# Softmax attention for one query, forward and backward: the block order of turns 3 to 14 used from turn 1 on

## The chip, the cores and the metric

The kernel runs on one core of a Trainium2 chip. The metric is device time in microseconds (us); lower is better. A core has TensorE (matrix products; PE in the profile, PEld its weight loads), VectorE (DVE), ScalarE (ACT), GpSimd (POOL), SyncE (SP), and data engines that move bytes between HBM and the on-chip memory SBUF. TensorE writes to PSUM, from which VectorE and ScalarE read.

## The reference

There are 32 heads, one query per head, 8192 keys and values per head, 128 wide, all in bf16.

```python
B, H, Sq, Skv, Dh = 1, 32, 1, 8192, 128
...
scores = jnp.einsum('bhqd,bhkd->bhqk', q, k) * scale
attn = _softmax(scores, axis=-1)
return jnp.einsum('bhqk,bhkd->bhqd', attn, v)
```

The outputs are this result and, for a given grad_out, the gradients of q, k and v. With p the softmax of one head, dV is the outer product of p and grad_out, dp is V times grad_out, ds is p times (dp minus the sum of p times dp) times the scale, dq is ds times K, and dK is the outer product of ds and q. So K and V (67 MB each) are read once, and dK and dV, as large, are written once.

## The kernel before, in words

A **turn** takes two heads: one tile of K and one of V, each 128 partitions by 128 rows by 128 values (4 MB). There are 16 turns, 0 to 15. Three SBUF buffers hold K and two hold V; dK and dV are written over K and V in place (`outer`, line 371) and stored from there. The order of the instructions on every engine is the order in which they are written, since the kernel has a manual schedule.

A turn t goes through these steps:

- `k_block(t, c)`, c from 0 to 7 (lines 196 to 209): VectorE transposes an eighth of K in blocks of 32 by 32 (line 200, into one of three buffers XK), and TensorE multiplies it by q in four matmuls of 512 columns (line 208), which add up the scores in PSUM. These blocks are done at the end of turn t - 1.
- `s_back`, `s_top`, `s_exp`, `s_sum`, `p_of` (lines 212 to 255): VectorE turns the scores back (sT, line 215), and the maximum, the exponentials and their sum go to and fro between VectorE, ScalarE and TensorE until p is there.
- dp from V. The old way is `v_part` (lines 260 to 279): TensorE transposes four squares of 128 by 128 (line 273, f32 words) into a PSUM bank, and ScalarE copies the bank to SBUF (line 279); 16 such parts make a turn, and `v_scores` (line 290) multiplies each quarter by grad_out in 8 narrow matmuls of 32 columns of weights. The other way is `v_block` (line 298): VectorE transposes an eighth of V in blocks of 32 by 32, and `v_wide` (line 310) multiplies it in four wide matmuls with the weights do_wide, which `weights_wide` (line 195, four copies on ScalarE) sets for each turn. Four blocks r = 0 to 3 and two quarters of `v_part` then make the whole of V.
- `contract(t, "p")` (line 349) multiplies p with V on TensorE, for the output.
- `v_back` (dpT, line 319), `pd_sum`, `ds_of` (lines 330 to 340): ds; ScalarE writes it to the window win_ds (line 244) that `contract(t, "ds")` uses as weights, to multiply ds with K for dq.
- `outer(t, "p", r)` writes dV, r from 0 to 7, in the same turn; `outer(t - 1, "ds", r)` writes dK of the turn before. Both are on VectorE, at line 371.
- Every fourth turn `gather` (lines 357 to 365) brings an output together: that of p in turns 3, 7, 11 and 15, that of ds in turns 4, 8 and 12 and at the end.

`wide(t)` (line 257) says which turns take the four blocks by VectorE: 3 to 14. It also chooses between two orders of a turn. In the order of **blocks** (from line 479 on) all of the eight multiplications for dK, and seven of those for dV, are done before dpT; the eighth stands between dpT and ds; the store of V is issued ahead of ds; then all of the eight `k_block` of the next turn follow. In the **other** order (turns 1, 2 and 15) 16 parts of V go by TensorE. Five of them are done beside `k_block` of the turn before: by line 464 for turn 1, and by the last lines of the loop for a turn that isn't wide. Two or three multiplications for dV stand before ds, and five after it. In turn 2 these five alternate with the `k_block` of turn 3; in turn 1 they stand ahead of those of turn 2. Turn 0 has an order of its own, in `first` (lines 406 to 465).

SP's queue holds all of the large transfers in this order: the store of K of turn t - 1, the store of V of turn t, the load of K of turn t + 2, the load of V of turn t + 2. Each waits for what it needs, and those behind it wait too. A load of K waits for the store of the dK that had its buffer, three turns back; a load of V for the store of dV two turns back.

Of the kernel before, what the change touches and what calls it, by code (L numbers as in the profile page):

```python
# [27 lines left out]
def kernel(  # L28
# [14 lines left out]
    HP = H // 2  # L43
# [39 lines left out]
    def load_k(t, parts=1):  # L83
        load(k, Kt, t, parts)

    def load_v(t, parts=1):
        load(v, Vt, t, parts)
# [40 lines left out]
    def copies(row):  # L128
        four = xkpool.tile([H, 2 * NW, NQ, QD], BF16, tag="XK", name="four")
        for w in range(NW):  # L130
            for e2 in range(2):
                nc.vector.tensor_copy(
                    four[:, 2 * w + e2],
                    rows[:, row, :].rearrange("h (w j e) -> h w e j", w=NW, e=2)[:, w, e2:e2 + 1, :]
                    .to_broadcast([H, NQ, QD]))
        return four

    def columns(four, cols):
        tp = psT.tile([P, 2 * TB, P], BF16, tag="T", name="tp_q")
        for c in range(2 * NW):  # L140
            nc.tensor.transpose(tp[:, c, 0:H], four[:, c].rearrange("h a j -> h (a j)"), ident[0:H, 0:H])
        for s in range(2):
            nc.vector.tensor_copy(
                cols[s * HF:(s + 1) * HF], tp[s * HF:(s + 1) * HF, 0:2 * NW, 0:H].rearrange(
                    "p c (i s) -> p s c i", s=2)[:, s])
# [42 lines left out]
    def weights_do(t):  # L188
        for z in range(2):
            nc.scalar.copy(do_win[z * W:(z + 1) * W, :, :, SL - 2 + z].rearrange("p s e -> p e s"),  # L190
                           do_cols[z * W:(z + 1) * W, :, 2 * t:2 * t + 2])

    def weights_wide(t):
        for a in range(NQ):
            nc.scalar.copy(do_wide[a * QD:(a + 1) * QD, :, a * QD + SL - 1], do_four[a * QD:(a + 1) * QD, :, t])
# [16 lines left out]
    def s_back(t):  # L212
        x = st[t]
        x["sT"] = backs.tile([P, BN, QD], F32, tag="back", name="sT")
        nc.vector.transpose(x["sT"][:].rearrange("p n r -> p (n r)"), x.pop("s")[:])  # L215

    def s_top(t):
        x = st[t]
        mx = small.tile([P, 1], F32, tag="mx")
        nc.vector.reduce_max(mx[:], x["sT"][:, :, 0:NB], axis=AX.XY)  # L220
        top = small.tile([P, 1], F32, tag="top")
        nc.vector.tensor_scalar_mul(top[:], mx[:], scale)  # L222
        nc.tensor.transpose(x["m"][:, 128:256], top[:].to_broadcast([P, P]), ident_f[:])  # L223

    def s_exp(t):
        x = st[t]
        nbias = small.tile([P, 1], F32, tag="nbias")
        for s in range(2):
            a, b = s * HF, (s + 1) * HF
            nc.vector.tensor_reduce(nbias[a:b], x["m"][a:b, 128 + a:128 + b], axis=AX.X, op=ALU.max, negate=True)  # L230
        e = x["e"] = single.tile([P, NT], F32, tag="e", name="e")
        rs = small.tile([P, 1], F32, tag="rs")
        nc.scalar.activation(e[:].rearrange("p (c n) -> p n c", c=NB), x["sT"][:, :, 0:NB], ACT.Exp, bias=nbias[:],  # L233
                             scale=scale, accum_out=rs[:])
        return rs

    def s_sum(t, rs):
        nc.tensor.matmul(st[t]["m"][:, 0:1], lhsT=same[:], rhs=rs[:], start=True, stop=True, skip_group_check=True)  # L238
# [8 lines left out]
    def p_of(t):  # L247
        x = st[t]
        rinv = x["rinv"] = small.tile([P, 1], F32, tag="rinv", name="rinv")
        nc.vector.reciprocal(rinv[:], x["m"][:, 0:1])  # L250
        x["p"] = single.tile([P, NT, R], BF16, tag="prep", name="p_rep")
        nc.scalar.activation(x["p"][:], x["e"][:].unsqueeze(2).to_broadcast([P, NT, R]), ACT.Copy, scale=rinv[:])
        window_in(t, "p", x["p"][:, :, 0])
        x["rs"] = small.tile([P, 1], F32, tag="rs_s", name="rinv_s")
        nc.scalar.mul(x["rs"][:], rinv[:], scale)

    def wide(t):
        return 3 <= t < HP - 1

    def v_bank(t, m):  # L260
        x = st[t]
        z, i = divmod(m, NM // TB)
        if t == 0:
            if i == 0:
                x["XV", z] = k_in[2][:].rearrange("p n d -> p (n d)").bitcast(F32).rearrange(
                    "p (z m s) -> p z m s", z=NZ, s=P)[:, z]
        elif i == 0:
            x["XV", z] = xvpool.tile([P, NM, P], F32, tag="XV", name="XV_sb")[:]
        T_ps = psT.tile([P, TB, P], F32, tag="T", name="T_ps")
        words = Vt[t][:].rearrange("p n d -> p (n d)").bitcast(F32)  # L270
        for j in range(TB):
            at = (i * TB + j) * NZ + z
            nc.tensor.transpose(T_ps[:, j, :], words[:, at * P:(at + 1) * P], ident_f[:])  # L273
        x["T", m] = T_ps

    def v_copy(t, m):
        x = st[t]
        z, i = divmod(m, NM // TB)
        nc.scalar.copy(x["XV", z][:, i * TB:(i + 1) * TB, :], x.pop(("T", m))[:])  # L279
# [46 lines left out]
    def pd_sum(t):  # L326
        x = st[t]
        nc.tensor.matmul(x["m"][:, 1:2], lhsT=same[:], rhs=x["pd"][:], start=True, stop=True, skip_group_check=True)  # L328
# [13 lines left out]
    def contract(t, which, first=0, last=NG):  # L342
        X, pool = (Vt[t], psO) if which == "p" else (Kt[t], psQ)
        if t % ST == 0 and first == 0:
            acc[which] = pool.tile([P, 512], F32, tag="acc", name="acc_" + which)
        at = 0 if which == "p" else (ST - 1 - t % ST) * SL
        for g in range(first, last):
            b = g % NQ
            nc.tensor.matmul(acc[which][b * QD:(b + 1) * QD, :], lhsT=win[which][:, g, at:at + QD],  # L349
                             rhs=X[:, 4 * g:4 * g + 4, :].rearrange("p n d -> p (n d)"),  # L350
                             start=(t % ST == 0 and g < NQ), stop=(t % ST == ST - 1 and g >= NG - NQ),
                             skip_group_check=True)
        if which == "p" and last == NG:
            nc.gpsimd.memset(win["p"][:, :, t % ST * SL:(t % ST + 1) * SL], 0.0)
# [12 lines left out]
    def outer(t, which, r):  # L367
        x = st[t]
        X, row = (Kt[t], 0) if which == "ds" else (Vt[t], 1)
        a, b = r * BN, (r + 1) * BN  # L370
        nc.vector.tensor_tensor(  # L371
            X[:, a:b, :].rearrange("p n (a b) -> p n a b", b=R),
            x[which][:, a:b, :].unsqueeze(2).to_broadcast([P, BN, D // R, R]),
            x["qd"][:, row, :].rearrange("p (a b) -> p a b", b=R).unsqueeze(1).to_broadcast([P, BN, D // R, R]),
            op=ALU.mult)
# [21 lines left out]
    def v_part(t, m):  # L397
        v_bank(t, m)
        v_copy(t, m)

    HALF = NB // 2
# [10 lines left out]
    def first():  # L412

        def at(i, *zs):
            return [z * (NM // TB) + i for z in zs]

        for m in at(0, 0, 1):
            v_part(0, m)
        s_back(0)
        s_top(0)  # L420
        for m in at(0, 2, 3):
            v_part(0, m)
        four = copies(1)
        rs = s_exp(0)
        for m in at(1, 0, 1, 2):
            v_bank(0, m)
        s_sum(0, rs)
        for m in at(1, 0, 1, 2):
            v_copy(0, m)
        p_of(0)  # L430
        ahead = at(1, 3) + at(2, 0, 1)
        for m in ahead:
            v_bank(0, m)
        contract(0, "p", 0, NG // 2)
        for m in ahead:
            v_copy(0, m)
        for r in range(HALF):
            outer(0, "p", r)
        for m in at(2, 2, 3):
            v_part(0, m)  # L440
        contract(0, "p", NG // 2, NG // 4 * 3)
        for r in range(HALF, NB - 2):
            outer(0, "p", r)
        for m in at(3, 0, 1, 2, 3):
            v_part(0, m)
        contract(0, "p", NG // 4 * 3, NG)
        for z in range(NZ):
            v_scores(0, z)
        weights_do(1)
        v_back(0)  # L450
        pd_sum(0)
        columns(four, do_four)
        outer(0, "p", NB - 2)
        ds_of(0)
        contract(0, "ds")
        prepare(1)
        outer(0, "p", NB - 1)
        store(0, "p")
        load_k(2)
        load_v(2)  # L460
        for c in range(NB):
            k_block(1, c)
            if c > HALF:
                v_part(1, c - HALF - 1)
        weights_q(2)

    first()
# [153 lines left out]
```

## Time and profile before

| what | value |
|---|---|
| time, median of 3 runs | 634.3 us (634.27 to 634.5) |
| profiled execution, time | 634.35 us |
| profiled execution, span | 632.5 us |
| VectorE busy | 550.5 us (87%) |
| TensorE matmul busy | 426.6 us (67%) |
| ScalarE busy | 176.2 us (28%) |
| moved by the data engines | 268.92 MB, mean 425 GB/s |
| mean granted clock of TensorE | 0.81 |

The span is the stretch from the first to the last event of the execution; the time has 1.85 us more around it. The granted clock is 1.0 where TensorE runs at full speed and 0.5 at half. The page of the profile gives shares of the whole span; the views that are cut by time show single turns. A wait is written as the idle time of an engine ahead of an instruction, with the instruction or transfer that ended it.

### The profile page before, as it was taken

Reading aid. Unit: us, or ns where it says so; the run is one execution under the profiler, and the core shown is the slowest. Engines: PE = TensorE matmul, PEld = TensorE weight load, DVE = VectorE, ACT = ScalarE, POOL = GpSimd, SP = SyncE. Lnnn points to the kernel's source line nnn. Section 1 sums busy time; section 2 is a strip of 40 time slices with the busy share of each in tenths; the row PEclk is TensorE's granted clock in tenths of the full one; section 3 lists DMA queues with packets and bytes.
Section 4 is the critical chain, followed back from the end, with each engine's and each line's share of the span. In section 5 each row is a group of like instructions: output and inputs, shape, how many; then the busy total and the mean of one; then the engine's idle time right before and its main releaser. Section 6 shows DMA issues by size and latency. Waiting matters only on the chain.

```text
span 632.5 us, 7251 instructions
## 1 busy us (share of the span) xinstructions
PE 426.6 (67%) x2876; PEld 207.7 (33%) x2876; DVE 550.5 (87%) x630; ACT 176.2 (28%) x439; POOL 9.2 (1%) x27
## 2 busy tenths in 40 slices
PE   5868686488475874758747587474875748757870
PEld 2635252144242421323323242231332314223540
DVE  8688987997988979899797997989979799798893
ACT  1616152041240322404124031240412304122530
POOL 2000000000000000000000000000000000000000
PEclk9989697787698776888868877687886878768965
DMA  8999999999999999999999999999999999999997
GB/s 361 434 418 433 431 430 430 433 432 430 431 430 430 434 424 435 428 435 432 434 443 430 429 432 432 428 431 432 431 428 431 430 431 432 430 432 432 411 407 310
DMA packets 11025, 268.92 MB, mean 425 GB/s; under 512 B 1392, under 2 KB 1392, under 8 KB 1392
## 3 DMA queue, kind: packets, MB, share of 16 engines
q1 hardware_dynamic: 10896, 268.46, 99.0%
q8 instruction: 22, 0.36, 0.2%
q14 instruction: 11, 0.09, 0.0%
q10 hardware_dynamic: 96, 0.02, 0.0%
HBM read 134.23 MB, written 134.23 MB: 424 GB/s over the span
## 4 chain that ended last, share of the span: by engine, by line
PE 41%; DVE 40%; issue 7%; ACT 6%; DMA 4%; DVEq 0%; ACTq 0%
DVE K L371 18%; PE T_ps L273 9%; PE dp_ps L310 9%; DVE XK_sb L200 9%; PE acc_ds L349 7%; PE acc_p L349 6%; PE s_ps L208 5%; DVE V L371 5%; DMA K<-in_k_dram 3%; PE dp_ps L290 3%; DVE XV_blk L298 2%; ACT XV_sb L279 2%; ACT win_ds L244 2%; DVE sT L215 2%; DVE dpT L319 1%
## 5 line engine op out<-in xcount | busy, mean ns | idle before, releaser
L200 DVE STREAM_TRANSPOSE XK_sb<-K 128x1024 f32<-128x1024 f32 x128 | 148.6, 1215 | 40.3 <-PE s_ps L208 37.9
L371 DVE TENSOR_TENSOR V<-p_rep,qd 128x2048 bf16<-128x2048 bf16 x128 | 150.8, 1219 | 7.6 <-PE T_ps L273 3.4
L371 DVE TENSOR_TENSOR K<-ds_rep,qd 128x2048 bf16<-128x2048 bf16 x128 | 149.2, 1211 | 0.5
L208 PE MATMUL s_ps<-XK_sb,q_win 128*128 128x512 bf16 x512 | 132.9, 404 | 9.9 <-DVE XK_sb L200 5.8
L279 ACT COPY XV_sb<-T_ps 128x512 f32<-128x512 f32 x144 | 78.2, 589 | 130.4 <-PE T_ps L273 130.3
L273 PE MATMUL T_ps<-ident_f,V 128*128 128x128 f32 x640 | 92.8, 293 | 0.1
L273 PEld LDWEIGHTS T_ps<-ident_f,V 128*128 128x128 f32 x640 | 75.3, 150 | 34.0 <-issue 26.6
L310 PE MATMUL dp_ps<-XV_blk,do_wide 128*128 128x512 bf16 x192 | 62.3, 454 | 31.2 <-DVE XV_blk L298 31.2
L208 PEld LDWEIGHTS <-q_win 128*128 128x128 bf16 x512 | 50.9, 102 | 85.0 <-issue 38.3
L349 PE MATMUL acc_ds<-K,win_ds 128*32 128x512 bf16 x512 | 52.9, 586 | 33.3 <-ACT win_ds L244 33.3
L298 DVE STREAM_TRANSPOSE XV_blk<-V 128x1024 f32<-128x1024 f32 x48 | 55.3, 1208 | 0.0
L223 PE MATMUL m_ps<-ident_f,top 128*128 128x128 f32 x16 | 6.7, 416 | 62.2 <-DVE top L222 62.2
L349 PE MATMUL acc_p<-V,win_p 128*32 128x512 bf16 x512 | 42.7, 428 | 1.6 <-ACT win_p L244 1.6
L310 PEld LDWEIGHTS <-do_wide 128*128 128x128 bf16 x192 | 19.9, 109 | 49.6 <-DVE XV_blk L298 32.2
L349 PEld LDWEIGHTS <-win_ds 128*32 128x32 bf16 x512 | 17.2, 130 | 56.1 <-ACT win_ds L244 31.2
L185 ACT COPY q_win<-q_blk 128x16 bf16<-128x16 bf16 x16 | 4.2, 261 | 108.7 <-PE s_ps L208 108.7
L233 ACT ACTIVATE e<-sT,nbias 128x128 f32<-128x128 f32 x16 | 8.2, 515 | 69.7 <-DVE nbias L230 69.7
L223 PEld LDWEIGHTS m_ps<-ident_f,top 128*128 128x128 f32 x16 | 2.7, 170 | 68.8 <-issue 62.2
L290 PE MATMUL dp_ps<-XV_sb,do_win 128*32 128x512 bf16 x288 | 20.8, 383 | 5.2 <-ACT XV_sb L279 5.0
L238 PE MATMUL m_ps<-rs,same 128*128 128x1 f32 x32 | 8.3, 327 | 18.1 <-ACT e L233 18.1
L244 ACT ACTIVATE win_ds<-ds,rinv_s 64x128 bf16<-64x128 f32 x32 | 12.8, 399 | 27.5 <-DVE ds L336 27.3
L328 PE MATMUL m_ps<-pd,same 128*128 128x1 f32 x32 | 6.1, 260 | 19.8 <-DVE m_ps L322 19.8
(68 smaller groups left out, 215.0 us busy)
## 6 DMA issues: line engine op xcount, KB each, us to landing
K<-in_k_dram SPq DMA_DIRECT2D x15, 4096.0 KB, 19.2
V<-in_v_dram SPq DMA_DIRECT2D x15, 4096.0 KB, 19.3
out_dram<-V SPq DMA_DIRECT2D x15, 4096.0 KB, 25.4
out_dram<-K SPq DMA_DIRECT2D x14, 4096.0 KB, 27.4
out_dram<-K SPq DMA_DIRECT2D x4, 2048.0 KB, 9.5
K<-in_k_dram SPq DMA_DIRECT2D x4, 1024.0 KB, 8.2
V<-in_v_dram SPq DMA_DIRECT2D x4, 1024.0 KB, 15.6
out_dram<-V SPq DMA_DIRECT2D x4, 1024.0 KB, 8.3
```

What stands on the lines that cost most here:

```text
L200: nc.vector.transpose(X[:], Kt[t][:, c * BN:(c + 1) * BN, :].rearrange("p n d -> p (n d)").bitcast(F32).rearrange("p (n w j) -> p n w j", ...
L208: nc.tensor.matmul(x["s"][:], lhsT=q_win[:, 2 * w + e2, SL - 1 - c:SL - 1 - c + P], rhs=cols[:, w, e2], start=(c == 0 and w == 0 and e2 == 0),
L215: nc.vector.transpose(x["sT"][:].rearrange("p n r -> p (n r)"), x.pop("s")[:])
L223: nc.tensor.transpose(x["m"][:, 128:256], top[:].to_broadcast([P, P]), ident_f[:])
L244: nc.scalar.activation(win[which][a:b, :, at + 4 * s:at + 4 * s + 4], src[a:b].rearrange("p (g j) -> p g j", j=4), ACT.Copy, scale=1.0 if ...
L273: nc.tensor.transpose(T_ps[:, j, :], words[:, at * P:(at + 1) * P], ident_f[:])
L279: nc.scalar.copy(x["XV", z][:, i * TB:(i + 1) * TB, :], x.pop(("T", m))[:])
L290: nc.tensor.matmul(x["dp"][b * QD:(b + 1) * QD, :], lhsT=do_win[:, b // 2, e2, at:at + QD], rhs=cols[:, e2, :, b * QD:(b + 1) * QD], start ...
L298: nc.vector.transpose(X[:], Vt[t][:].rearrange("p n d -> p (n d)").bitcast(F32).rearrange("p (m r w j) -> p m r w j", r=SL, w=NW, j=QD)[:, ...
L310: nc.tensor.matmul(st[t]["dp"][:], lhsT=do_wide[:, 2 * w + e2, at:at + P], rhs=cols[:, w, e2], start=(r == 0 and w == 0 and e2 == 0), stop ...
L349: nc.tensor.matmul(acc[which][b * QD:(b + 1) * QD, :], lhsT=win[which][:, g, at:at + QD], rhs=X[:, 4 * g:4 * g + 4, :].rearrange("p n d -> ...
L371: nc.vector.tensor_tensor(X[:, a:b, :].rearrange("p n (a b) -> p n a b", b=R), x[which][:, a:b, :].unsqueeze(2).to_broadcast([P, BN, D // ...
```

## The change: turns 1 and 2 become wide

```diff
     def wide(t):
-        return 3 <= t < HP - 1
+        return 1 <= t < HP - 1
...
         columns(four, do_four)
+        weights_wide(1)
         outer(0, "p", NB - 2)
         ds_of(0)
...
         for c in range(NB):
             k_block(1, c)
-            if c > HALF:
-                v_part(1, c - HALF - 1)
         weights_q(2)
```

Turns 1 and 2 take four V blocks by VectorE and half of V by TensorE, in the order of blocks. The weights do_wide of turn 1 are set in turn 0, those of turn 2 at the end of the V work of turn 1. The five parts of V of turn 1 beside `k_block(1, c)` go; so do, by the condition at the end of the loop, the five of turn 2 beside `k_block(2, c)`. The eight `k_block` of turn 3 no longer alternate with multiplications for dV. The transfers stay the same, and so does their order in SP's queue.

## The prediction

> **What bounds the kernel now.** I read the transfers first, since the page shows them full.
>
> ```profile
> DMA  8999999999999999999999999999999999999997
> q1 hardware_dynamic: 10896, 268.46, 99.0%
> ```
>
> The data engines are busy 99% of the span, so it looks as if nothing but bytes could count. But a full queue sets the end only if the engines that compute wait for it. So next the waits of VectorE (engine, tile and line, waited for, us in total, times, longest):
>
> ```profile
> DVE XK_sb L200 <- PE s_ps L208: 37.9, 17, 4.6
> DVE XK_sb L200 <- DMA K<-in_k_dram: 2.4, 1, 2.4
> ```
>
> VectorE waits for a load once after the start, 2.4 us, and for TensorE 37.9 us. The third view is VectorE's timeline, which says where (start, length, line, operation, count, then the idle time before it):
>
> ```profile
> 47.27 3.46 DVE L371 TENSOR_TENSOR K<-ds_rep,qd 128x2048 bf16<-128x2048 bf16 x3
> ...
> 81.30 3.46 DVE L371 TENSOR_TENSOR K<-ds_rep,qd 128x2048 bf16<-128x2048 bf16 x3
> ...
> 103.43 1.25 DVE L200 STREAM_TRANSPOSE XK_sb<-K 128x1024 f32<-128x1024 f32 x1 [2.43 <-DMA K<-in_k_dram]
> ...
> 117.02 4.59 DVE L371 TENSOR_TENSOR K<-ds_rep,qd 128x2048 bf16<-128x2048 bf16 x4
> ```
>
> A turn begins with the dK multiplications of line 371 on K of the turn before. Turns 1, 2 and 3 begin at 47.27, 81.30 and 117.02. K of turn 3 is awaited at 103.43, in turn 2. From there the chain that ended last holds no transfer until the final stores: it runs over VectorE and TensorE. So 103.43 is the last place where compute has slack, 2.4 us of it; whatever delays the start of turn 3 goes on to the end. The fourth view is the table by stages, cut at the starts of the turns 1 to 14 (stage, length, busy PE, PEld, DVE, ACT, POOL, granted clock, DMA share, GB/s):
>
> ```profile
> 47.27:81.30 34.03, 25.46 (x199) 13.89 (x198) 30.61 (x36) 12.37 (x29) 0.31 (x1) 0.85 1.01 435
> 81.30:117.02 35.72, 26.52 (x198) 13.73 (x196) 30.46 (x36) 13.13 (x33) 0.31 (x1) 0.86 1.00 428
> 117.02:157.80 40.78, 28.09 (x176) 13.71 (x175) 35.35 (x40) 10.49 (x27) 0.31 (x1) 0.79 1.01 435
> 157.80:197.34 39.54, 26.82 (x176) 12.74 (x175) 35.36 (x41) 10.61 (x27) 0.31 (x1) 0.83 1.00 428
> 197.34:237.24 39.90, 27.28 (x168) 12.13 (x167) 35.26 (x41) 9.86 (x25) 0.31 (x1) 0.74 1.00 430
> 237.24:275.14 37.90, 25.27 (x168) 11.31 (x167) 34.99 (x41) 9.75 (x25) 0.31 (x1) 0.82 1.01 433
> 275.14:314.23 39.09, 26.20 (x176) 12.47 (x175) 34.90 (x40) 10.39 (x27) 0.31 (x1) 0.83 1.01 435
> 314.23:354.08 39.85, 27.14 (x176) 12.87 (x175) 35.34 (x40) 10.61 (x27) 0.31 (x1) 0.83 1.01 433
> ```
>
> This is the view that decides. Turns 1 and 2, in the old order, take 34.03 and 35.72; every turn in the new order takes 37.9 to 40.8. Its VectorE is busy 35 us instead of 30.5. The four turns from 3 on repeat: the turns 7 to 10 are 39.09, 39.85, 40.11 and 37.92 (157.0 together), the turns 11 to 14 39.13, 39.86, 40.10 and 37.93. So there are six turns without a gather to copy from: 5, 9 and 13 take 39.90, 40.11 and 40.10, and 6, 10 and 14 take 37.90, 37.92 and 37.93.
>
> **The change part by part.**
>
> *Four V blocks by VectorE (line 298), in turns 1 and 2.* The group is x48 at 1208 ns, so 4 x 1.21 = 4.8 us a turn; the stages show 35.26 - 30.61 = 4.65. VectorE sets the pace, so I cost it in full: 9.2 us in two turns.
>
> *What goes from TensorE and ScalarE.* A turn loses 32 transposes (line 273, 293 ns: 9.4 us), 8 copies (line 279, 589 ns: 4.7 us) and 16 narrow matmuls (line 290, 383 ns), and gains 16 wide ones (line 310, 454 ns: 7.3 us). VectorE hardly waited for these: the five parts after k_block(1) hide in turn 1 beside 5.75 us of transposes that follow one another without idle time. I cost their going at nothing.
>
> *The order.* Now in turn 1 five V multiplications (5.76 us) stand between ds and k_block(2), and TensorE does contract(ds) beside them. In the new order one multiplication stands there, so the fourth transpose of K waits until TensorE is through: 2.3 to 4.6 us idle in turns 3 to 14, against 0.6 in turn 1 now. Turn 2 also has the 2.43 us for K; in the new order k_block(3) begins near 114, 11 us after K has landed, so that wait goes and cannot pay for anything more.
>
> *Turn by turn.* Which of the six rows fits turn 1? Up to its start nothing changes. The clock record of the trace falls to half 4.5 us after the start of turn 5 and 5.5 after turn 6. Its steps come 3.4 us apart, and those near turn 1 stand at 41.4, 44.8, 48.2, 51.6; TensorE ends k_block(1) at about 48.3, so its first whole step without work ends at 51.6, 4.3 after the start: turn 5's case. I take 40.0 for turn 1 (+6.0) and 37.9 for turn 2 (+2.2). Turn 3 then begins at 125.2, 8.2 late. Turn 3, now 40.78, should be like turns 7 and 11, 39.1 (-1.7); turns 4 and 5 like 8 and 9 (+0.5). Turn 15 is reached 6.0 + 2.2 - 1.7 + 0.5 = 7.0 us late. Bounds: a turn is not below VectorE's busy 35.3 plus the 1.5 us idle that turn 1 has least (1.2 in k_block(1), 0.3 before dpT), 36.8, and not above turn 3's 40.8. That is +3.9 to +11.9 before, and +2.7 to +11.9 after, what turns 3 to 5 give.
>
> *weights_wide(1).* Four copies on ScalarE (206 ns: 0.8 us) behind the copy of do_four, which ends at 34.05. Behind them stands win_ds, which waits for ds until 35.99: 1.1 us to spare, so nothing; uncovered, 0.8.
>
> *SP's queue.* The order of transfers stays. The store of K0 moves to 47.3 + 15.4 (turn 3's distance) = 62.7 from 60.10, that of V1 to 73.8 from 71.53, K1 to 102.7 from 94.20, V2 to 113.8 from 112.59. What the queue still holds then (bytes issued less bytes moved by the trace's packets, at 431 GB/s) is 13.8, 12.3, 18.9 and 10.2 us, more than each delay; from turn 3 to 14 it is never under 12.1 us when a store is issued. So the engines don't run dry before turn 15, and the loads land as now.
>
> *The end.* In turn 15 the queue is short. The last 4.2 MB, two halves of K, now begin at
>
> ```profile
> 617.99 0.33 SPq L381 DMA_DIRECT2D out_dram<-K  x1
> ...
> 622.53 0.35 SPq L381 DMA_DIRECT2D out_dram<-K  x1
> ```
>
> and end at 632.5, 14.5 later: by the trace's packets some 0.7 of queue in front, 2.1 from issue to the first packet, 9.7 of transfer, 2.0 at the end. 7.0 late, the quarters of V have gone before, and the 0.7 falls away: +6.3.
>
> The sum: the profiled execution, 634.35 (its span 632.5 and 1.85 around it; the median is 634.3), plus 6.3 is **640.6 us**.
>
> **The rivals.**
>
> *Another clock step* (0.28). The steps come 3.4 us apart and the four-turn rhythm of 157.0 is 46 of them, so a lateness could settle one step off. Downwards: TensorE at full clock through both turns, 36.8 each, about 3.4 less: 637.2. For it: the clock near turn 1 is granted for 27 us. Against: TensorE idles after k_block in this order, and each turn that has it falls to half. Upwards: both turns near 40, or turn 3 as slow as now: 644.0. I give 0.10 and 0.18.
> [...]
>
> *The transfers set the end* (0.05). If the stores' queue covers the delay to the last, the time stays at 634.3. For it: 99% and over 12 us of queue until turn 14. Against: in turn 15 the DMA share falls to 0.8 in several 2 us slices, and the last store follows line 371.
> [...]
>
> *Faster: the rhythm falls by one step* (0.04). One mechanism, in turns 3 to 14: started at another phase, four turns could lock at 45 steps, 153.6. Three rounds would give back 10 us, more than 6.3, and the transfers would bind (four turns move 67.1 MB, 155.7 us at 431 GB/s). The end then loses the 2.0 us that the data engines idle from 594 to 628: 632.4. It decides from 2.1 us a round. Against: two rounds agree within 0.05 us.
>
> *It doesn't do what it says* is excluded: the instruction order of the changed kernel has the new turns.
>
> **How the numbers follow.** The forecast has 0.63 (639 to 642). The range takes in the clock steps, 636.8 to 644.4; left out are the two cases without loss, the rest of the bounds, some 0.15. A measurement tells about 0.2%, 1.3 us: slower 0.91, same 0.05, faster 0.04.
>
> **What would show it.** Turns 1 and 2 of 40 and 38 us, with 35 of VectorE; no wait of line 200 for K; idle time before the fourth transpose of K of 2.3 us or more; turn 3 from 125 on, and 39 long; the last store issued at 629.5. Wrong it is if turns 1 and 2 stay below 36 us (then little is lost), or if later turns change their rhythm.

## The result, and the profile after

The changed kernel takes 639.7 us in the median of 6 executions (639.16 to 644.55) against 634.3 (633.38 to 634.5): a ratio of 1.0099, interval 1.008 to 1.0119. It is slower, about as far as forecast (640.6). Five executions took 639.2 to 640.2 and one 644.55, at a mean granted clock of 0.795 instead of 0.805 to 0.81. The profiled execution took 640.07 with a span of 638.3.

The page of the changed kernel, the same two lines as before:

```profile
DMA  8999999999999999999999999999999999999698
q1 hardware_dynamic: 10896, 268.46, 98.2%
```

The data engines are full until the 37th of 40 slices; the 6 in the 38th is new. The stages of the changed kernel, cut at the starts of turns 1 to 6 (stage, length, busy PE, PEld, DVE, ACT, POOL, granted clock, DMA share, GB/s):

```profile
47.61:87.50 39.89, 27.27 (x168) 12.11 (x167) 35.26 (x41) 9.87 (x25) 0.31 (x1) 0.74 1.00 432
87.50:125.40 37.90, 25.28 (x168) 11.30 (x167) 34.99 (x41) 9.77 (x25) 0.31 (x1) 0.82 1.00 429
125.40:164.50 39.10, 26.22 (x176) 12.49 (x175) 34.90 (x41) 10.41 (x27) 0.31 (x1) 0.83 1.01 432
164.50:204.33 39.83, 27.11 (x176) 12.90 (x175) 35.34 (x40) 10.62 (x27) 0.31 (x1) 0.83 1.01 433
204.33:244.44 40.11, 27.48 (x168) 12.13 (x167) 35.26 (x40) 9.86 (x25) 0.31 (x1) 0.74 1.00 431
```

Turns 1 and 2 have become copies of turns 5 and 6 of the kernel before, down to busy times and clock; turn 3, begun 8.4 us late, is 39.10 long and not 40.78. Turn 15 starts at 596.77 instead of 589.13. VectorE's only wait for K (2.4 us) is gone; its wait for TensorE at line 200 is 42.1 us instead of 37.9.

From the start of turn 15 to the end, the span has 41.5 us instead of 43.4. SP's timeline shows the last two halves of K:

```profile
625.63 0.33 SPq L381 DMA_DIRECT2D out_dram<-K  x1
...
630.17 0.35 SPq L381 DMA_DIRECT2D out_dram<-K  x1
```

Both are issued 7.6 us later than before (617.99, 622.53), but the span ends 5.8 us later.

The view that says most about the cause is the chain that ended last, in turn 1 (start, length, engine, tile, line, count):

```profile
57.42 1.15 DVE XV_blk L298
58.62 1.89 PE dp_ps L310 x4
60.51 0.97 PE acc_p L349 x8
61.48 1.90 PE T_ps L273 x8
63.38 1.42 PE dp_ps L310 x4
64.80 0.55 PE acc_p L349 x8
65.34 1.03 PE T_ps L273 x8
...
70.85 0.59 ACT XV_sb L279
71.48 1.13 PE dp_ps L290 x14
72.63 0.73 DVE dpT L319
```

One V block of VectorE stands in it, 1.15 us, and then 14 us of TensorE's work on V, the first pieces, at half clock, nearly twice as long as the later ones (1.90 against 1.03 for the same eight transposes). The prediction had put four V blocks on the path.

### The profile page after: what moved, and what is told of

It is laid out like the page before. It is cut to its first block, busy times and chain, and to the rows that moved or that the text cites. A ratio compares the mean times of both kernels' runs of the same rounds, so it can differ in the third digit from the quotient of the medians.

```text
span 638.3 us, 7119 instructions
## 1 busy us (share of the span) xinstructions
PE 424.8 (67%) x2812; PEld 201.5 (32%) x2812; DVE 557.5 (87%) x638; ACT 170.6 (27%) x431; POOL 9.3 (1%) x27
## 4 chain that ended last, share of the span: by engine, by line
PE 43%; DVE 41%; issue 7%; ACT 6%; DMA 1%; DVEq 0%; ACTq 0%
DVE K L371 19%; PE dp_ps L310 10%; PE T_ps L273 10%; DVE XK_sb L200 8%; PE acc_ds L349 8%; PE acc_p L349 6%; DVE V L371 4%; PE s_ps L208 4%; PE dp_ps L290 3%; DVE XV_blk L298 3%; ACT win_ds L244 2%; ACT XV_sb L279 2%; DVE sT L215 2%; DVE dpT L319 1%; PE m_ps L363 1%
## 5 line engine op out<-in xcount | busy, mean ns | idle before, releaser
L200 DVE STREAM_TRANSPOSE XK_sb<-K 128x1024 f32<-128x1024 f32 x128 | 148.1, 1214 | 42.1 <-PE s_ps L208 42.1
L208 PE MATMUL s_ps<-XK_sb,q_win 128*128 128x512 bf16 x512 | 127.4, 391 | 4.9 <-ACT q_win L185 0.6
L279 ACT COPY XV_sb<-T_ps 128x512 f32<-128x512 f32 x128 | 69.5, 589 | 119.0 <-PE T_ps L273 119.0
L310 PE MATMUL dp_ps<-XV_blk,do_wide 128*128 128x512 bf16 x224 | 73.0, 455 | 36.4 <-DVE XV_blk L298 36.4
L273 PE MATMUL T_ps<-ident_f,V 128*128 128x128 f32 x576 | 85.4, 297 | 0.1
L273 PEld LDWEIGHTS T_ps<-ident_f,V 128*128 128x128 f32 x576 | 68.5, 151 | 33.5 <-issue 30.0
L298 DVE STREAM_TRANSPOSE XV_blk<-V 128x1024 f32<-128x1024 f32 x56 | 64.5, 1208 | 0.0
L349 PE MATMUL acc_p<-V,win_p 128*32 128x512 bf16 x512 | 44.6, 436 | 1.1 <-ACT win_p L244 1.1
L310 PEld LDWEIGHTS <-do_wide 128*128 128x128 bf16 x224 | 23.4, 110 | 58.2 <-DVE XV_blk L298 37.6
L290 PE MATMUL dp_ps<-XV_sb,do_win 128*32 128x512 bf16 x256 | 17.9, 384 | 4.1 <-ACT XV_sb L279 4.0
L252 ACT ACTIVATE p_rep<-e,rinv 128x512 bf16<-128x512 f32 x16 | 11.6, 727 | 29.9 <-DVE rinv L250 29.9
```

What stands on the lines that cost most here:

```text
L200: nc.vector.transpose(X[:], Kt[t][:, c * BN:(c + 1) * BN, :].rearrange("p n d -> p (n d)").bitcast(F32).rearrange("p (n w j) -> p n w j", ...
L208: nc.tensor.matmul(x["s"][:], lhsT=q_win[:, 2 * w + e2, SL - 1 - c:SL - 1 - c + P], rhs=cols[:, w, e2], start=(c == 0 and w == 0 and e2 == 0),
L290: nc.tensor.matmul(x["dp"][b * QD:(b + 1) * QD, :], lhsT=do_win[:, b // 2, e2, at:at + QD], rhs=cols[:, e2, :, b * QD:(b + 1) * QD], start ...
L298: nc.vector.transpose(X[:], Vt[t][:].rearrange("p n d -> p (n d)").bitcast(F32).rearrange("p (m r w j) -> p m r w j", r=SL, w=NW, j=QD)[:, ...
L310: nc.tensor.matmul(st[t]["dp"][:], lhsT=do_wide[:, 2 * w + e2, at:at + P], rhs=cols[:, w, e2], start=(r == 0 and w == 0 and e2 == 0), stop ...
```

## The experiments

The theory on record was that VectorE's V blocks, 9.2 us in two turns, are the cost and that compute carries it to the end. Against it stood the transfers and, in the expectations below, the order alone. Each ratio is to runs of the kernel before on the same chip (634.0 to 634.3 in the median); the stages are those of the one profiled execution, whose time stands beside them. A turn's length differs between executions even where its code doesn't: turn 1 takes 33.42 to 34.19 in the four rows that leave turns 1 and 2 as they were.

| kernel | turn 1 + turn 2 | turn 3 | start of turn 15 | profiled execution | median | ratio to before (95% interval) |
|---|---|---|---|---|---|---|
| before | 34.03 + 35.72 = 69.75 | 40.78 | 589.13 | 634.35 | 634.3 | 1 |
| changed | 39.89 + 37.90 = 77.79 | 39.10 | 596.77 | 640.07 | 639.69 | 1.0099 (1.008 to 1.0119) |
| turn 2 only | 33.39 + 38.44 = 71.83 | 41.72 | 591.85 | 635.11 | 635.11 | 1.0034 (1.0012 to 1.0056) |
| turn 1 only | 37.65 + 33.18 = 70.83 | 41.73 | 590.59 | 634.17 | 635.48 | 1.0022 (1.0012 to 1.0032) |
| changed, one V transpose of four | 39.75 + 37.86 = 77.61 | 39.08 | 595.93 | 639.21 | 639.44 | 1.0083 (1.0066 to 1.01) |
| before, V blocks unused | 38.42 + 38.28 = 76.70 | 41.76 | 595.47 | 638.28 | 638.28 | 1.0063 (1.0032 to 1.0093) |
| changed, one store less | 39.77 + 37.88 = 77.65 | 39.08 | 596.47 | 639.74 | 639.28 | 1.0082 (1.0067 to 1.0097) |
| before, one store less | 34.05 + 35.37 = 69.42 | 40.94 | 589.47 | 632.35 | 632.94 | 0.9983 (0.9973 to 0.9993) |
| changed, TensorE kept busy | 36.56 + 35.72 = 72.28 | 42.37 | 594.81 | 637.62 | 636.51 | 1.004 (1.0025 to 1.0055) |
| same, one V transpose of four | 34.76 + 34.77 = 69.53 | 40.76 | 588.96 | 633.85 | 634.43 | 1.0005 (0.9993 to 1.0018) |
| changed, parts ahead | 37.31 + 37.41 = 74.72 | 42.48 | 596.29 | 639.5 | 640.2 | 1.0093 (1.0076 to 1.0109) |
| same, one V transpose of four | 35.38 + 36.78 = 72.16 | 41.72 | 595.78 | 639.07 | 636.91 | 1.0045 (1.0028 to 1.0063) |
| before, TensorE kept busy in 3 to 14 | 34.19 + 34.84 = 69.03 | 37.04 | 583.92 | 636.81 | 636.23 | 1.0035 (1.0022 to 1.0048) |
| before, parts ahead in 3 to 14 | 33.42 + 35.27 = 68.69 | 41.68 | 583.13 | 636.34 | 636.57 | 1.0034 (1.0021 to 1.0047) |

**One turn alone.** Turn 2 only, as an edit to the kernel before:

```diff
-        return 3 <= t < HP - 1
+        return 2 <= t < HP - 1
```

> Only turn 2 takes the four blocks and their order; turn 1 stays as before. Theory (VectorE's work and its wait for contract, carried to the end by compute): turn 1 34.0 us, turn 2 37.9 to 40.0 with no wait for K of turn 3, which has landed 5 us before; turn 3 starts 2.2 to 4.3 us later than before and the time is 635 to 638. Rival (the later stores of turn 1 and 2 cost it, half for each turn): 637.0 with idle data engines before turn 15.

Measured: 635.1 (634.05 to 639.43 in ten executions). Turn 2 is 38.44, VectorE no longer waits for K, turn 3 starts 3.2 us late (120.18).

Turn 1 only, as an edit to the changed kernel:

```diff
-        return 1 <= t < HP - 1
+        return t == 1 or 3 <= t < HP - 1
```

> Only turn 1 takes the four blocks and their order; turn 2 stays in the old order. Theory: turn 1 39.9 us, turn 2 33.3 (its 35.7 less the 2.4 us wait for K, which is gone); turn 3 starts 3.6 us later than before, the time is 636 to 638. Rival (half of the loss for each turn): 637.0; rival (the slack of 2.4 us is not there): turn 2 35.7, turn 3 6.0 later, 639.

Measured: 635.5 (634.17 to 636.77), a little under the expected 636 to 638. The profiled execution is the fastest of the ten. In it turn 1 took 37.65 and not 39.9: it began at 48.12, and the clock was at half for 10.2 us (51.7 to 61.9) instead of 13.7 (50.7 to 64.4 in the changed kernel). Turn 2 took 33.18: the old order without its wait for K. Either turn alone adds 0.2 to 0.3%, both together 1%. By the stages the two turns are 2.08 and 1.08 us longer with one turn changed, 8.04 with both. Of the 4.88 us between, 2.4 are the wait for K, which each kernel gets back once; 2.2 are turn 1's 37.65 instead of 39.89, with its other clock.

**VectorE's transposes away.** An edit to the changed kernel:

```diff
-            for r in range(3):
+            for r in range(1 if t < 3 else 3):
                 v_block(t, r)
+            for r in range(1, 4 if t < 3 else 1):
+                st[t]["XW", r] = st[t]["XW", 0]
...
-                    v_block(t, 3)
+                    if t >= 3:
+                        v_block(t, 3)
```

> The changed kernel, but in turns 1 and 2 only the first of the four V blocks is transposed and used four times: the other three are left out of the computation, 3.6 us of VectorE a turn; order, matmuls and transfers stay. Theory: VectorE paces the turns, so turns 1 and 2 get 2.5 to 3.6 us shorter each and the time falls to 633.5 to 636. Rival (the order alone costs it, VectorE then waits longer for TensorE): the time stays at 639.3 within 1.

Measured: 639.4, as the changed kernel. This is the run against the theory. Its stages of turns 1 and 2, and VectorE's largest wait in the two (waited for, us, times, longest):

```profile
46.98:86.73 39.75, 27.13 (x168) 12.12 (x167) 31.87 (x37) 9.85 (x25) 0.31 (x1) 0.74 1.01 434
86.73:124.59 37.86, 25.24 (x168) 11.29 (x167) 31.87 (x38) 9.75 (x25) 0.31 (x1) 0.82 1.00 431
```

```profile
DVE V L371 <- PE T_ps L273: 7.0, 3, 3.4
```

VectorE has 6.5 us less to do in the two turns (31.87 and 31.87 against 35.26 and 34.99), and they get 0.18 shorter. It waits instead: 7.0 us for TensorE to be through with V before dV may be written over it, where the changed kernel waits 0.8.

**VectorE's transposes in the old order.** An edit to the kernel before:

```diff
                 p_of(t)
+                for r in range(4 if t < 3 else 0):
+                    v_block(t, r)
                 v_copy(t, 9)
```

> The kernel before in its old order, but in turns 1 and 2 VectorE also transposes four V blocks that nothing uses (4.8 us a turn). Theory: 9.6 us of VectorE less the 2.4 us wait for K make turn 3 up to 7 us late; time 637 to 641. Rival (the old order has 3.4 and 2.8 us of idle time that take the blocks in, only the new order costs): 634 to 636.

Measured: 638.3 (635.4 to 640.4). The two turns take 76.70, 6.95 more: 9.6 less the 2.4 for K is 7.2. So in the old order the V blocks do cost what they take, as far as this one execution shows it (two of the five took 635.4 and 636.1, three 638.3 to 640.4). In the new order three of the four cost 0.18 us in the two turns, because something longer runs beside them.

**One store less.** An edit to both kernels:

```diff
-        if blocks:
+        if blocks and t != 6:
             store(t, "p")
```

> The changed kernel without the store of dV of turn 6 (4.2 MB, 9.7 us of all 16 data engines; this part of the output is not written). Theory (compute carries the delay to the end): 638 to 639.5, and the queue runs dry more at the end. Rival (the transfers, 98% busy, set the end): 630.

> The kernel before without the store of dV of turn 6 (4.2 MB; this part of the output is not written). Theory: compute sets the end here too, so 632 to 634, only what the last stores wait behind others. Rival (the transfers, 99% busy, set the end): 624.6.

Measured: 639.3 for the changed kernel, as with the store (639.7), and 632.9 for the kernel before, 1.1 less. If the transfers set the end, both would be 9.7 us shorter (4.2 MB at 431 GB/s). With data engines that are busy 98 and 99% of the span, 9.7 us of their work are worth 0.4 us (within the spread) and 1.1 us of time.

**TensorE kept busy.** In turns 1 and 2 of the changed kernel, 31 matmuls with unused results stand where TensorE waits:

```diff
+    def keep_busy(t, n):
+        if 1 <= t < 3:
+            x = psD.tile([P, 512], F32, tag="dp", name="busy_ps")
+            for _ in range(n):
+                nc.tensor.matmul(x[:], lhsT=ident[:], rhs=do_wide[:].rearrange("p c j -> p (c j)")[:, 0:512],
+                                 start=True, stop=True, skip_group_check=True)
...
             s_back(t)
+            keep_busy(t, 12)
             s_top(t)
+            keep_busy(t, 5)
...
             s_sum(t, rs)
+            keep_busy(t, 8)
...
         pd_sum(t)
+        if blocks:
+            keep_busy(t, 6)
```

> The changed kernel with 31 more matmuls of 512 columns a turn in turns 1 and 2, in the places where TensorE waits (into a PSUM bank that is free, results unused). Theory (the half clock after TensorE's idle stretches sets what a turn takes above VectorE's 35.3 us): the clock stays at full there, turns 1 and 2 take 36.8 to 38 instead of 39.9 and 37.9, the time is 636 to 638. Rival (the clock isn't what costs): turns as long as now or up to 4 us longer, 639 to 645.

Measured: 636.5, and the stages from turn 1 to turn 3:

```profile
48.50:85.06 36.56, 31.23 (x197) 13.73 (x198) 35.02 (x41) 9.75 (x25) 0.31 (x1) 0.91 1.01 433
85.06:120.78 35.72, 30.07 (x197) 13.38 (x198) 34.80 (x41) 9.76 (x25) 0.31 (x1) 0.95 0.99 427
120.78:163.15 42.37, 29.59 (x176) 14.15 (x175) 35.37 (x41) 10.48 (x27) 0.31 (x1) 0.72 1.00 431
```

More work on TensorE makes the two turns 5.5 us shorter: the granted clock is 0.91 and 0.95 instead of 0.74 and 0.82, and now VectorE is busy nearly throughout (35.02 of 36.56). But turn 3, which has no added matmuls, takes 42.37 instead of 39.10, and so 3.3 of the 5.5 are given back. So the clock is part of the cause.

The same with one V transpose of four in these turns (both edits above):

> The changed kernel with the added matmuls of 512 columns in turns 1 and 2 and only one of the four V transposes there (three left out of the computation). New theory: with TensorE at full clock, VectorE's transposes set the turns, so taking them away now shortens what they didn't shorten at half clock: 634 to 635.8, against 636.5 with the added matmuls alone. Rival (transposes cost nothing at any clock): 636.5.

Measured: 634.4, the time of the kernel before (ratio 1.0005, interval 0.9993 to 1.0018), with turns of 34.76 and 34.77. At nearly full clock (0.91 to 1.00 in these stages) the same transposes are worth 2.75 us in the two turns (72.28 to 69.53); at 0.74 and 0.82 they were worth 0.18.

**TensorE's parts of V ahead of p.** An edit to the changed kernel, in turns 1 and 2:

```diff
             dk(0, 4)
+            ahead = [z * (NM // TB) + i for i in range(4) for z in range(2)] if t < 3 else []
+            for m in ahead[0:4]:
+                v_part(t, m)
             s_back(t)
             s_top(t)
+            for m in ahead[4:6]:
+                v_part(t, m)
             dk(4, 5)
             rs = s_exp(t)
+            for m in ahead[6:8]:
+                v_bank(t, m)
             s_sum(t, rs)
+            for m in ahead[6:8]:
+                v_copy(t, m)
...
-                for z in range(2):
+                for z in range(0 if ahead else 2):
                     v_part(t, z * (NM // TB) + i)
```

> The changed kernel, but in turns 1 and 2 TensorE does its eight parts of V ahead of p (four before the maximum, four around the sum), not after it. New theory: in the new order two chains of about one length stand side by side after p, VectorE's (blocks and multiplications) and TensorE's (all of V, begun at half clock after 10 us of waiting); here only TensorE's gets shorter, so VectorE sets turns of 36 to 37.5 us and the time is 636 to 637.5. Rival (VectorE alone paced the turns all along): 639 to 640.

Measured: 640.2. By its time this is a miss, and it is the time that the rival had; by its stages it is half a miss: turns 1 and 2 take 37.31 and 37.41, 3.1 less together, and VectorE doesn't wait before dpT any more. But turn 3 takes 42.48, 3.4 more than in the changed kernel, and turn 15 starts within 0.5 of where it did. What the two turns win is lost in the third.

With one V transpose of four as well:

> As the run with the parts ahead, and of the four V blocks in turns 1 and 2 only the first is transposed and used four times (three are left out of the computation). New theory: both chains are shorter now, turns 1 and 2 take 33 to 35 us, K of turn 3 may be awaited again, the time is 633.5 to 635.5. Rival (VectorE's transposes cost nothing): as the run with the parts ahead.

Measured: 636.9; turns of 35.38 and 36.78, longer than expected. The transposes are worth 2.6 us here. The profiled execution, at 639.07, isn't at the median, and its turns 3 and 4 take 41.72 and 41.11; the time of this run is no good measure of its two turns.

**Faster turns everywhere.** The added matmuls in turns 3 to 14 of the kernel before (the edit above, with `3 <= t < 15`), and the parts ahead in the same turns (with `True` for `t < 3`):

> The kernel before with the same 31 matmuls a turn in turns 3 to 14. Theory: at full clock these turns fall from 39.3 us to 36.8 to 38.9, less than the 38.9 that their 16.8 MB take, so the transfers bind at the end: 632 to 633. Rival (the added matmuls stand in the way of the maximum and the sum): 636 to 645.

> The kernel before with the eight parts ahead of p in turns 3 to 14. New theory: these turns fall from 39.3 us to 36 to 37.5 by compute, so VectorE waits for loads of K in each turn and the data engines end the run. If they end one by one over some 8 us, as with the added matmuls in all turns, 635 to 637; if they end together, 632 to 633.5.

Measured: 636.2 and 636.6, both slower than before, though turn 15 starts 5 to 6 us earlier (583.92 and 583.13). With the matmuls, VectorE's view of waits now reads

```profile
DVE XK_sb L200 <- DMA K<-in_k_dram: 38.3, 11, 5.0
```

so here the transfers do bind, as expected, but the end isn't at 632 to 633. The last 10 us of that run (stage as above; DMA share and GB/s are the last two columns):

```profile
625.00:627.00 2.00, 0.00 (x0) 0.00 (x0) 0.00 (x0) 0.00 (x0) 0.00 (x0) 0.50 0.77 328
627.00:629.00 2.00, 0.00 (x0) 0.00 (x0) 0.00 (x0) 0.00 (x0) 0.00 (x0) 0.50 0.39 164
629.00:631.00 2.00, 0.00 (x0) 0.00 (x0) 0.00 (x0) 0.00 (x0) 0.00 (x0) 0.50 0.12 49
631.00:633.00 2.00, 0.00 (x0) 0.00 (x0) 0.00 (x0) 0.00 (x0) 0.00 (x0) 0.50 0.06 25
633.00:635.00 2.00, 0.00 (x0) 0.00 (x0) 0.00 (x0) 0.00 (x0) 0.00 (x0) 0.50 0.02 8
```

The 16 data engines stop one after the other over 8 us (their last packets end from 625.8 to 633.7). The run with the parts ahead ends likewise (0.79, 0.50, 0.15, 0.06 and 0.02 in its last 10 us), though there VectorE still waits mostly for TensorE. No version that does all of the work beats the kernel before.

## Why the prediction was right, and where its reasoning was not

**Turn by turn: right, and in part by luck.** 40.0 and 37.9 were taken from rows of turns in the same order, and 39.89 and 37.90 were measured; turn 3 at 125.2 (125.40), 39.1 long (39.10), turns 4 and 5 39.83 and 40.11. The clock falls to half 3.1 us after the start of turn 1 for 13.7 us, as after that of turn 5 in the kernel before. The luck is that the clock's steps lie differently in each execution: turn 1 begins 0.3 to 0.6 us after a step in five of the eight profiled executions that have it in the new order, as turn 5 does in the kernel before (0.3), but 2.2 to 3.3 us after one in the other three. A start 2.1 us after a step gave turn 5 a length of 38.18 (turn 2 only, turn 1 only), not 40. One thing in that step was read wrongly: the prediction set the clock's steps and the packets against the instructions 1.3 us too late. Compared turn with turn that falls out, but half clock comes at 50.7, 1.9 us after k_block(1) ends, and not after a whole step without work (the step from 47.31 to 50.72 holds 1.35 us of TensorE's work); and each queue figure in the prediction is 1.3 us too long, which leaves 8.9 to 17.5 us at the four stores, still more than their delays.

**"VectorE sets the pace, so I cost it in full": wrong.** This was the step on the four V blocks, 9.2 us. In the new order three of the four cost 0.18 in the two turns (the run with one transpose of four). Beside the wait for `contract(ds)` the prediction put nothing on TensorE's side of the two turns, and there the longer chain is. In the old order TensorE has its first five parts of V behind it when a turn begins and goes on with V while the maximum and the sum are worked out; in turn 1 of the kernel before it waits 1.8 us for the maximum. In the new order all of V comes after p. TensorE waits 4.7 us for the maximum, falls to half clock at 50.7, and begins V at 58.6; the chain from there to dpT is TensorE's. TensorE's wait for the maximum in turn 1, before and after (waited for, us, times, longest):

```profile
PE m_ps L223 <- DVE top L222: 1.8, 1, 1.8
```

```profile
PE m_ps L223 <- DVE top L222: 4.7, 1, 4.7
```

The total came out right because it was read from whole turns, which hold both chains; the split of it was a guess. The chain view of the kernel before had the answer in its turns 3 to 14: each has one piece of line 298 there, 1.15 us, and then TensorE's.

What the runs show in its place: two chains side by side, TensorE's the longer at the clock it gets (0.74 and 0.82). Take three of VectorE's four blocks away, and the two turns change by 0.2; bring TensorE to nearly full clock, and they lose 5.5, until VectorE's chain sets them; do both, and they lose 8.3 and are 69.5, as in the old order (69.75). In the old order, VectorE's blocks alone cost 6.95. Either half of the change costs nearly all of the 8.04 us that both cost: 6.95 for the blocks without the order, 7.86 for the order with one block.

**The order: right in size.** Idle time before the fourth transpose of K was to be 2.3 or more: 3.14 in turn 1 and 2.29 in turn 2.

**weights_wide(1): right.** ScalarE's timeline of the changed kernel:

```profile
34.04 0.86 ACT L195 COPY do_wide<-do_four 32x4 bf16<-32x4 bf16 x4 [2.00 <-DVE do_four L143]
36.21 0.81 ACT L244 ACTIVATE win_ds<-ds,rinv_s 64x128 bf16<-64x128 f32 x2 [1.32 <-DVE ds L336]
```

It ends at 34.90, and win_ds still waits 1.32 for ds.

**SP's queue: right.** The stores moved to 63.08, 74.85, 102.97 and 113.60 (62.7, 73.8, 102.7 and 113.8 expected), and K of turn 3 was asked for at 83.91 (84.16 before).

**The end: mis-sized.** Two errors partly cancel here. Turn 15 starts 7.64 late, not 7.0: 0.34 of it are there at the start of turn 1, and turns 11 to 14 take 157.4 instead of 157.0. The end was to give 0.7 back and gave 1.8. The last 4 us of the changed kernel:

```profile
634.30:636.30 2.00, 0.00 (x0) 0.00 (x0) 0.00 (x0) 0.00 (x0) 0.00 (x0) 0.50 0.92 393
636.30:638.30 2.00, 0.00 (x0) 0.00 (x0) 0.00 (x0) 0.00 (x0) 0.00 (x0) 0.50 0.02 8
```

All of the 16 data engines end between 636.4 and 637.0; in the kernel before, 15 ended from 628.8 to 629.8 and the last at 631.2. The queue had run short in turn 15 (share 0.47 from 602 to 606); that the engines that were behind caught up there is my guess, which no run tests. The prediction had let the queue ahead of the last stores shrink by 0.7, and kept the end of the engines as it was.

**The rivals.** That the transfers set the end was refuted by the two runs with one store less. The upward clock step is what the one execution at 644.55 looks like (644.0 was given for it), but it has no profile here. The faster rhythm didn't come: in all kernels whose turns 3 to 14 are as before, the four turns from 6 on take 156.9 to 157.2. It does exist: with the parts ahead in turns 3 to 14, turns 6 to 9 take 153.94 and turns 10 to 13 153.62, where the prediction had 153.6 for it. Its time of 632.4 wasn't reached there (636.6); the data engines ended one after the other.

**Why turn 3 gives back what turns 1 and 2 win.** In the clock records of the kernel before and of the changed kernel, every change in the span (57 and 61) falls on steps 3.413 us apart, and the steps lie elsewhere in each execution (0.45 us later in the changed kernel). Twelve kernels (all but the last two rows of the table) have the same code in turns 3 to 14, but for the one store in two of them. In them the length of turn 3 goes with the time from the last step to its start:

| start of turn 3 after a step | kernels | turn 3 |
|---|---|---|
| 0.2 to 0.4 us | parts ahead; TensorE kept busy | 42.48; 42.37 |
| 1.5 to 1.9 us | before; before, one store less; TensorE kept busy, one transpose | 40.78; 40.94; 40.76 |
| 2.2 to 2.7 us | turn 2 only; turn 1 only; V blocks unused; parts ahead, one transpose | 41.72; 41.73; 41.76; 41.72 |
| 3.0 us | changed; one transpose; changed, one store less | 39.10; 39.08; 39.08 |

For the changed kernel, for example, the clock falls at 50.72; 21 steps of 3.413 later is 122.40, and turn 3 begins at 125.40. What turn 2 held doesn't show: 41.72 after the new order and 41.73 after the old. At the end of turn 3 the clock is at half for 10.2 us in the run with parts ahead (149.2 to 159.5) and for 3.4 in the changed kernel (153.1 to 156.5), and the idle time before the fourth transpose of K is 5.49 and 3.66 us. By turn 7 all of the twelve start 3.0 to 3.1 us after a step, and that turn takes 39.06 to 39.10. From the first step in the span up to there it is 79 steps in the kernel before, its run with one store less and the run with added matmuls and one transpose, 80 where one turn alone was changed, and 81 in the others. So what turns 1 and 2 win or lose arrives at turn 7 as whole steps: the 5.5 us of the run with added matmuls are 1.9 there (280.45 against 282.38), and those only because the steps lie 1.96 us earlier in that execution: both are 81 steps in.

The stretches of half clock are whole steps long in these traces (3.4, 6.8, 10.2 and 13.7 us). No run varied TensorE's work in a single step by itself. Of stretches with transposes these traces show the following: in turn 1 of the kernel before, 4.0 of the 4.8 us that TensorE works between 48.6 and 55.2 are transposes of line 273, and full clock lasts to 67.3. The step from 53.68 to 57.09 holds 3.30 us of TensorE's work, 2.60 of it transposes, and full clock follows; the step from 63.92 to 67.33 holds 0.93 us of work without transposes, and half clock follows.

## What to carry to other kernels

Take a step's cost from whole stages that already have the new form, with their waits, before you split it; where you split it, follow the chain view and charge an engine only with what stands in it, for of two chains side by side the longer hides the shorter (here all but 0.18 of VectorE's 6.5 us). Work that one engine can do before a result is known (here TensorE's transposes ahead of p) can also go with a higher clock of the engine: in turn 1 the granted clock was then 0.86 instead of 0.74, and its first stretch at half 3.4 us (53.7 to 57.1) instead of 13.7 (50.7 to 64.4); in turn 2 it was 0.77 instead of 0.82. But look at the later stages before you count the gain: where the clock changes in steps, here 3.413 us apart, the stages can settle on whole steps, and here more than half of the gain (3.3 of 5.5 us) was lost in the next turn. And a resource that is 99% busy need not be the bound (9.7 us of the transfers' work were worth 0.4 and 1.1 us here): take some of its work away and see.

## What the runs showed of the hardware that was not expected

- **More matmuls, less time.** 62 added matmuls of 512 columns made the two turns 5.5 us shorter; the granted clock rose from 0.74 and 0.82 to 0.91 and 0.95.
- **The data engines don't end together.** In the run with TensorE kept busy in turns 3 to 14, where the queue stayed full to the end (DMA share 0.98 or more from 600 to 624), the 16 engines ended from 625.8 to 633.7; in the changed kernel, with the same bytes, where it ran short before the last stores (0.47 from 602 to 606), they ended within 0.6 us of each other. So the kernel with the faster turns was slower, by 0.35%.
- **Turns settle on the clock's steps.** In twelve profiled executions, whatever turns 1 and 2 held, turn 7 began 3.0 to 3.1 us after a step of 3.41 us, 79, 80 or 81 steps into the run.
